# Order of the first transfers and a smaller activity credit in an attention and state-space kernel

## The chip, the core and the metric

The kernel runs on one NeuronCore of one Trainium2 chip. The metric is the device time of one execution in microseconds (us). Engine names are those of the profile: PE is the matrix engine, PEld its weight loads, DVE the vector engine, ACT the scalar engine, POOL and SP the other two. SP and ACT also issue transfers (DMAs); their issue rows are called SPq and ACTq.

## The reference

```python
g = sigmoid((x * gate_w).sum(-1, keepdims=True))          # x: 1 x 2048 x 512, bf16
# a: softmax attention with 32 heads of 16
q, k, v = split(x @ wqkv)
p = softmax(einsum("bhqd,bhkd->bhqk", q, k) * 16 ** -0.5)
a = einsum("bhqk,bhkd->bhqd", p, v) @ wo
# b: state-space convolution, 512 channels, 128 complex states each
dt = exp(log_dt);  A = A_re + 1j * A_im
K = einsum("dn,dnl,dn->dl", C, exp(dt * A * l), dt * B).real
b = causal_convolution(x, K) + x * Dskip                    # the reference uses an FFT
out = g * a + (1 - g) * b
```

## The kernel before

**Tiles and groups.** Attention is 32 heads by 16 key tiles (of 128 keys) by 4 query chunks (of 512 queries), which makes 2048 score tiles of 128 keys by 512 queries. They are worked off in 683 groups of three. For group `g`, `qk(g)` on PE writes the scores into one of two score buffers in PSUM (`SC0`, `SC1`); `ex(g)` on ACT takes the exponential of two or three of the tiles and writes them to `ET`; where ACT takes two, DVE makes the third by integer arithmetic on the bit pattern (`DZ`, `DU`). `pv(q)` on PE multiplies four finished tiles with the values (`VE`) into the PSUM bank `OA`. All other work stands between these: projections of later heads into the bank `MB`, the tables and the convolution kernel of the state-space part (DVE, PE), the convolution itself (PE), the normalization and the output product.

**What sets the order.** Each engine runs its instructions in the order in which `record` writes them, and waits on semaphores for what they need. A planner in `record` decides that order while it writes: it keeps an estimated clock for each engine, and after each `ex(g)` its method `fill` issues pieces of the other work that fit before the next group. Transfers have no planner: SP and ACT issue theirs in the order of the program.

**Activity and the fill.** The planner counts for PE how many columns the matmuls stream, weighted by the share of the 128x128 array that they use: a 512-column matmul on the whole array counts 512, one on a quarter of it (32 rows or 32 columns: `qk`, `pv`) counts 128. For each group it wants `FILL` = 1300 such columns per 1.335 us of ACT's estimated time. What is missing is made up by matmuls with a zero operand (`wm`), which add nothing: `zero` writes four of them side by side, of 512 or 256 columns each, into the accumulation bank in use (rows `OA<-wm` or `MB<-wm`), or into the next score buffer (`SC<-wm`). What a group has over or under its want is passed to the next in `lack`, within limits (lines of the kernel before):

```python
1607        t = p.tm["ACT"]
1608        want = FILL * (t - t0) / 1.335 + min(max(lack, -256), 768)
1609        t0 = t
1610        sch.fill(t, t + OVER, want)
1611        lack = want - p.act
1612        p.act = bare = 0
1613        while lack >= 256 and p.tm["PE"] < t + OVER:
1614            z = zbank()
1615            if z is None:
1616                bare = BARE
1617                break
1618            n = 512 if lack >= 512 else 256
1619            for j in range(4):
1620                zero(z, n, (0, 32 * j), 128, 32, n * ZCOL if j == 0 else 0, n // 4, "C")
1621            lack -= n
```

A negative `lack` is a surplus. Since less than 256 missing columns bring no fill, a surplus of 256 lets the next group run 256 plus almost 256 columns under 1300.

**The start.** `x0n` is the first quarter of x (512 rows, 512 KB), with rows on partitions; `ldt` is log_dt, repeated on all partitions; `Wq`, `Wk`, `Wv` are the parts of wqkv; `AimT`, `AreT`, `BreT` ... are the state-space parameters, transposed by the transfer; `xT` is x transposed, its chunks 1 to 3 by transposing transfers. Chunk 0 is made on PE: 16 matmuls `SC<-idb,x0n` and `MB<-idb,x0n` transpose `x0n`, and four copies (`CAST xT`, quarters `q4` = 0 to 3) bring it to `xT`, two on DVE and two on ACT. Before and after these PE runs 9 and 5 matmuls on zeros (`OA<-wm`, `SC<-wm` 128x512). Then come `bn` = `AimT` * `dt` and `ba` on DVE, the sine and cosine `sb_` and `cb` on ACT, the first projections (`OA<-xT,Wq`, `SC<-xT,Wk`), their copies (`Qm`, `KT`) on DVE, and `qk(0)`. ACT changes its function table for `dt` (exponential), `sb_` (sine) and the first `ET` (exponential).

The profile's lines 647 and 651 are those of the helpers `mm` and `load`, 662 and 666 those of `load_xT` and `load_par`, 928 that of `ex`, 964 that of `bits`. In the changed kernel all lines behind line 47 stand one lower, so 647 becomes 648.

Of the kernel before, what the change touches and what calls it, by code (L numbers as in the profile page):

```python
# [10 lines left out]
AF = mybir.ActivationFunctionType  # L11
ALU = mybir.AluOpType

P = 128
S = 2048
D = 512
# [28 lines left out]
RATE = 24.0  # L45
BURST = 48
FILL = 1300
OVER = 0.3
DLAG = .6
TURN = dict(F=.105, R=.105, C=.105, H=.06)  # L50
# [57 lines left out]
class Prog:  # L108
# [139 lines left out]
    def dma(self, eng, fn, R=(), W=(), c=.45, lat=3.0, m=DMARG):  # L248
        if self.cap is not None:
            self.cap.append((self.dma, (eng, fn, R, W), dict(c=c, lat=lat, m=m)))  # L250
            return
        self.log.append((self.dma, self.q, (eng, fn, R, W)))
        if eng == "POOL":
            k = NDSEM + self.pnext
            self.pnext = (self.pnext + 1) % NPSEM
        else:
            k = self.dnext
            self.dnext = (k + 1) % NDSEM
        s = ("D", k)
        deps = self._deps(s, R, W)  # L260
        if self.dn[k]:
            deps[s] = max(deps.get(s, -1), self.dn[k])
        at = self.tm[eng]
        for s2, k2 in deps.items():
            at = max(at, self.fin[(s2, k2)] + .08)
        self.tm[eng] = at + c
        self.dn[k] += 1
        self.fin[(s, self.dn[k])] = at + c + lat
        self.marg[(s, self.dn[k])] = m
        self._record(eng, fn, deps, s, self.dn[k], R, W)  # L270
# [352 lines left out]
def dap(t, off, dims):  # L623
    return bass.AP(tensor=t, offset=off, ap=[list(d) for d in dims])
# [6 lines left out]
def record(nc, p, B, ins):  # L631
# [6 lines left out]
    op, dma = p.op, p.dma  # L638
# [3 lines left out]
    x_t, w_t = ins["x"], ins["w"]  # L642
    MM, QUAD = .23, .22

    def mm(out, lhsT, rhs, R, W, start=True, stop=True, pos=None, c=MM, a=512, cfg="F"):
        kw = {} if pos is None else dict(tile_position=pos)
        op("PE", lambda t: t.matmul(out(), lhsT(), rhs(), start=start, stop=stop, skip_group_check=True, **kw), R, W,  # L647
           c=c, lat=.15, a=a, cfg=cfg)

    def load(eng, b, src, W, dims=None, off=0, c=.5, lat=4.5):  # L650
        dma(eng, lambda e: e.dma_start(b(off, dims), src()), [], W, c=c, lat=lat)
# [10 lines left out]
        dma("SP", lambda e: e.dma_start_transpose(xT(512 * c, [[S, 4], [1, 512]]),  # L662
                                                  dap(x_t, 512 * c * D, [[D, 512], [1, D]])), [], [(xT, c)], c=5.4, lat=1.5)

    def load_par(n, src, q="SP"):
        dma(q, lambda e: e.dma_start_transpose(B[n](0, [[1, D]]), src), [], [(B[n], 0)], c=1.25, lat=2.5)

    def load_w(n, c0, at, cols, sl, eng="ACT"):
        load(eng, B[n], lambda: dap(w_t, c0 + at, [[3 * D, P], [P * 3 * D, 4], [1, cols]]), [(B[n], sl)], [[D, 4], [1, cols]], at)

    load("SP", B["x0n"], lambda: dap(x_t, 0, [[D, P], [P * D, 4], [1, D]]), [(B["x0n"], 0)], [[D, 4], [1, D]])
    load("ACT", B["ldt"], lambda: dap(ins["ldt"], 0, [[0, P], [1, D]]), [(B["ldt"], 0)], [[1, D]])
    load_w("Wq", 0, 0, P, 0)
    load_w("Wk", D, 0, P, 0, "SP")
    load_par("AimT", ins["aim"])
    load_par("AreT", ins["are"])
    load_w("Wv", 2 * D, 0, D, 0, "SP")
    load_xT(1)
    load_w("Wk", D, P, D - P, 1, "SP")
# [11 lines left out]
    idf, idb, x0n = B["idf"], B["idb"], B["x0n"]  # L691
# [160 lines left out]
    def acts(g):  # L852
        return len(slots(g)) - (vec[g][2] if g in vec else 0)
# [31 lines left out]
    def at_slot(s):  # L885
        q, j = divmod(tiles[s], 4)
        b, kt = divmod(q, 16)
        return q, j, b, kt, (b % 8) // 2
# [136 lines left out]
    def key(*ns):  # L1025
        return [(B[n], 0) for n in ns]
# [499 lines left out]


    mb, oa = (MB, 0, 0), (OA, 0, 0)
    op("ACT", lambda a: a.activation(B["dt"](0, [[1, D]]), B["ldt"](0, [[1, D]]), AF.Exp), key("ldt"), key("dt"), c=.6)
    for q4 in range(4):  # L1530
        sc = SC[1] if q4 < 3 else MB
        off = 512 * (q4 % 3)
        sl = q4 % 3
        for i in range(4):
            mm(lambda sc=sc, off=off, i=i: sc(off + 128 * i, [[1, P]]), lambda q4=q4, i=i: x0n(D * i + P * q4, [[1, P]]),
               lambda: idb(0, [[1, P]]), [(x0n, 0), (idb, 0)], [(sc, sl, 'x0')], c=.07)
        R, W = [(sc, sl, 'x0')], [(xT, (0, q4))]
        if q4 % 2:
            op("ACT", lambda v, sc=sc, off=off, q4=q4: v.copy(xT(q4 * S, [[1, 512]]), sc(off, [[1, 512]])), R, W, c=.58)
        else:  # L1540
            op("DVE", lambda v, sc=sc, off=off, q4=q4: v.tensor_copy(xT(q4 * S, [[1, 512]]), sc(off, [[1, 512]])), R, W, c=.62)
    for k in range(5):
        mm(lambda: SC[0](512, [[1, 512]]), lambda: wm(0, [[1, 128]]), lambda: wm(0, [[1, 512]]), [(wm, 0)], [(SC[0], 1, "warm")])
    tt("DVE", full("bn"), full("AimT"), full("dt"), ALU.mult, key("AimT", "dt"), key("bn"), F5)
# [23 lines left out]
    def need(g):  # L1568
        for s in slots(g):
            q, j, b, kt, pi = at_slot(s)  # L1570
            sch.force(f"K{pi}.{kt // 4}")
            sch.force(f"qm{b}")

    ring = {}
    lack = t0 = bare = 0
    for g in range(NG):
        p.q = g
        if g == GKEEP:
            for n in ("gT", "zc"):
                B[n].last = g  # L1580
        for i in range(acts(g)):
            if held[g] + i in ring:
                sch.force(f"pv{ring[held[g] + i] // 4}")
            ring[held[g] + i] = tiles[3 * g + i]
        ex(g)
        sch.mark(f"g{g}")
        sch.mark(f"blk{at_slot(3 * g)[2]}")
        if g + 1 < NG:
            decide(g + 1)
            need(g + 1)  # L1590
            if g - 1 in vec:
                sch.force(f"bits{g - 1}")
            sc = SC[(g + 1) % 2]
            while lack >= 256 and bare:
                n = 512 if lack >= 512 else 256
                for j in range(4):
                    zero((sc, [(sc, 0, ("z", g + 1))]), n, (0, 32 * j), 128, 32, n * ZCOL if j == 0 else 0, n // 4, "C", True)
                lack -= n
                bare -= 1
            lack += p.act  # L1600
            qk(g + 1)
            if g + 1 in vec:
                i = sets[vec[g + 1][0]]["old"]
                if i is not None:
                    sch.force(f"dvp{i}")
                sch.add(bits(g + 1), 0)
        t = p.tm["ACT"]
        want = FILL * (t - t0) / 1.335 + min(max(lack, -256), 768)
        t0 = t
        sch.fill(t, t + OVER, want)  # L1610
        lack = want - p.act
        p.act = bare = 0
        while lack >= 256 and p.tm["PE"] < t + OVER:
            z = zbank()
            if z is None:
                bare = BARE
                break
            n = 512 if lack >= 512 else 256
            for j in range(4):
                zero(z, n, (0, 32 * j), 128, 32, n * ZCOL if j == 0 else 0, n // 4, "C")  # L1620
            lack -= n
        p.act = 0
# [24 lines left out]
    for i in range(4):  # L1647
        b, off, sl = banks[i]
        R, W = [(b, sl, ('o', 12 + i))], [(fo, i, 12 + i)]
# [39 lines left out]
```

## Time and profile before

| | |
|---|---|
| median of 3 runs | 809.06 us (807.52 to 810.83) |
| the profiled execution | 809.1 us, its span 807.3 us |
| mean granted clock of PE | 0.973 |
| busy in the span | ACT 780.6 us (97%), DVE 728.8 (90%), PE 696.1 (86%), PEld 277.2 (34%), POOL 11.7 |
| exponentials | 683 instructions, 772.1 us |

All times are counted from the start of the span. The profiled execution took as long as the median of the runs, within 0.1 us; 1.8 us of it lie outside the span. ACT is busy nearly all the time, so the places to look at are those where it is not: the start, the end and short waits between. A row of a timeline gives start, duration, engine, line, operation, output<-input and, in brackets, how long the engine sat idle before it and for what. A row of the stretches gives for each engine the busy time and the number of instructions, then the granted clock of PE (1.00 is full), the DMA share and GB/s.

### The profile page before, as it was taken

Reading aid. Unit: us, or ns where it says so; the run is one execution under the profiler, and the core shown is the slowest. Engines: PE = TensorE matmul, PEld = TensorE weight load, DVE = VectorE, ACT = ScalarE, POOL = GpSimd, SP = SyncE. Lnnn points to the kernel's source line nnn. Section 1 sums busy time; section 2 is a strip of 40 time slices with the busy share of each in tenths; the row PEclk is TensorE's granted clock in tenths of the full one; section 3 lists DMA queues with packets and bytes.
Section 4 is the critical chain, followed back from the end, with each engine's and each line's share of the span. In section 5 each row is a group of like instructions: output and inputs, shape, how many; then the busy total and the mean of one; then the engine's idle time right before and its main releaser. Section 6 shows DMA issues by size and latency. Waiting matters only on the chain.

```text
span 807.3 us, 27243 instructions
## 1 busy us (share of the span) xinstructions
PE 696.1 (86%) x12164; PEld 277.2 (34%) x12164; DVE 728.8 (90%) x1355; ACT 780.6 (97%) x695; POOL 11.7 (1%) x15
## 2 busy tenths in 40 slices
PE   7897878787788877778889999999999989999986
PEld 2322323323222434444434443443343432222221
DVE  5889999999699999989897889898989999999994
ACT  6999999999999999999999999999999999999995
POOL 5000000000000000000000000000000000000000
PEclk9969998999999999999999999999999999999999
DMA  8900000100531988877767899979897931000000
GB/s 193 166 2 17 9 15 15 30 12 14 152 105 44 208 193 214 205 172 185 205 145 177 211 225 202 207 179 178 190 188 160 181 74 29 19 17 24 18 7 28
DMA packets 115125, 93.17 MB, mean 115 GB/s; under 512 B 77760, under 2 KB 90432, under 8 KB 115008
## 3 DMA queue, kind: packets, MB, share of 16 engines
q1 hardware_dynamic: 114048, 90.91, 49.5%
q8 instruction: 95, 1.56, 0.9%
q10 hardware_dynamic: 960, 0.52, 0.3%
q14 instruction: 22, 0.18, 0.1%
HBM read 70.88 MB, written 13.97 MB: 105 GB/s over the span
## 4 chain that ended last, share of the span: by engine, by line
ACT 82%; PE 11%; DVE 4%; issue 1%; DMA 1%; ACTq 0%
ACT ET L928 82%; PE SC L647 5%; PE OA L647 3%; PE MB L647 3%; DVE DZ L964 1%; DMA x0n<-in_A_x_dram 1%; DVE PT L1020 0%; DVE ft L1020 0%; DVE ta L1020 0%; DVE KT L737 0%; DVE DZ L975 0%; DVE FP L1020 0%; DVE Yst L1337 0%; DVE At L1158 0%; DVE Kst L1245 0%
## 5 line engine op out<-in xcount | busy, mean ns | idle before, releaser
L928 ACT ACTIVATE ET<-SC 128x1024 bf16<-128x1024 f32 (+1 forms) x683 | 772.1, 1434 | 11.3 <-PE SC L647 6.9
L647 PE MATMUL SC<-Qm,KT 32*128 32x512 bf16 x2048 | 280.8, 391 | 85.8 <-ACT ET L928 72.5
L964 DVE TENSOR_SCALAR DZ<-SC 128x512 uint16<-128x512 f32 x348 | 230.2, 684 | 19.6 <-PE SC L647 18.8
L647 PE MATMUL OA<-ET,VE 128*32 128x512 bf16 x1700 | 170.6, 399 | 0.9 <-ACT ET L928 0.8
L647 PEld LDWEIGHTS SC<-Qm,KT 32*128 32x128 bf16 x2048 | 72.3, 91 | 269.2 <-ACT ET L928 232.2
L647 PE MATMUL OA<-wm 32*128 32x512 bf16 (+3 forms) x524 | 142.7, 389 | 1.2 <-DVE wm L695 1.2
L647 PE MATMUL MB<-Xop,Kf 128*64 128x64 bf16 (+1 forms) x4096 | 108.5, 196 | 3.9 <-issue 3.5
L647 PEld LDWEIGHTS MB<-Xop,Kf 128*64 128x64 bf16 (+1 forms) x4096 | 87.0, 104 | 51.1 <-issue 40.6
L647 PEld LDWEIGHTS OA<-ET,VE 128*32 128x32 bf16 x1700 | 43.0, 94 | 94.5 <-issue 90.5
L975 DVE TENSOR_SCALAR DZ<-DZ 128x2048 uint16<-128x2048 uint16 x87 | 59.4, 683 | 9.1 <-PE OA L647 9.0
L975 DVE TENSOR_SCALAR DU<-DZ 128x2048 uint16<-128x2048 uint16 x87 | 58.4, 684 | 0.2
L647 PEld LDWEIGHTS OA<-wm 32*128 32x128 bf16 (+2 forms) x524 | 34.6, 94 | 7.5 <-issue 6.2
L647 PE MATMUL OA<-DZ,VS 128*32 128x512 bf16 x348 | 34.8, 386 | 0.9 <-DVE DZ L975 0.9
L647 PE MATMUL OA<-DZ,VE 128*32 128x512 bf16 x348 | 34.3, 382 | 0.0
L647 PE MATMUL OA<-DU,VS 128*32 128x512 bf16 x348 | 34.3, 383 | 0.0
L647 PEld LDWEIGHTS MB<-PT,At 128*32 128x32 bf16 x2048 | 25.1, 95 | 10.3 <-issue 3.8
L647 PE MATMUL MB<-PT,At 128*32 128x64 bf16 (+1 forms) x2048 | 27.3, 189 | 0.3 <-issue 0.3
L1337 DVE TENSOR_TENSOR Yst<-MB,gt 128x512 bf16<-128x512 f32 x32 | 21.9, 684 | 4.8 <-PE MB L647 4.7
L1020 DVE TENSOR_TENSOR FP<-ft,ft 128x128 f32<-128x128 f32 (+1 forms) x64 | 22.8, 357 | 1.8
L999 DVE STREAM_TRANSPOSE OT<-OA 128x512 f32<-128x512 f32 x32 | 22.7, 710 | 1.7 <-PE OA L647 1.3
L647 PE MATMUL MB<-xT,Wk 128*128 128x512 bf16 x60 | 20.3, 428 | 0.3 <-DVE Kst L1245 0.3
L647 PE MATMUL MB<-Wv,xT 128*128 128x128 bf16 x256 | 20.3, 227 | 0.0
(227 smaller groups left out, 531.8 us busy)
## 6 DMA issues: line engine op xcount, KB each, us to landing
Xop<-gm_xpd SPq DMA_DIRECT2D x64, 320.0 KB, 4.7
Xop<-gm_xpd SPq DMA_DIRECT2D x64, 316.0 KB, 4.8
Kf<-gm_kpd SPq DMA_DIRECT2D x32, 376.0 KB, 5.4
Kf<-gm_kpd SPq DMA_DIRECT2D x32, 369.0 KB, 5.2
gm_ytd<-Yst SPq DMA_DIRECT2D x32, 128.0 KB, 4.2
gm_kpd<-Kst SPq DMA_DIRECT2D x32, 94.0 KB
gm_qd<-Qs SPq DMA_DIRECT2D x15, 128.0 KB, 1.7
Qm<-gm_qd SPq DMA_DIRECT2D x120, 16.0 KB, 3.3
```

Source lines behind the costliest of these rows:

```text
L647: op("PE", lambda t: t.matmul(out(), lhsT(), rhs(), start=start, stop=stop, skip_group_check=True, **kw), R, W, c=c, lat=.15, a=a, cfg=cfg)
L928: op("ACT", lambda a: a.activation(ET(512 * e, [[1, 512 * n]]), sc(0, [[1, 512 * n]]), AF.Exp, scale=DH ** -0.5), [(sc, i, g) for i in ran ...
L964: op("DVE", lambda v: v.tensor_scalar(z.u16(512 * k, [[1, 512 * n]]), sc(512 * na, [[1, 512 * n]]), XS, XBI, ALU.mult, ALU.add), [(sc, na ...
L975: op("DVE", lambda v: v.tensor_scalar(t.u16(0, [[1, 2048]]), z.u16(0, [[1, 2048]]), float(STEP[k][0]), None, ALU.add), R, W, c=.07 + 2048 ...
L999: op("DVE", lambda v: v.transpose(OT(512 * w, [[1, 512]]), OA(0, [[1, 512]])), [(OA, 0, b)], [(OT, w, b)], c=.64)
L1020: op(eng, lambda v: v.tensor_tensor(o(), a(), b_(), f), R, W, c=c)
L1337: op("DVE", lambda v, r2=r2: v.tensor_tensor(Yst(r2 * 512, [[64, 8], [1, 64]]), MB(0, [[64, 8], [1, 64]]), B["gt"](0, [[0, 8], [1, 64]]), ...
```

## The change

It has two parts. The first is the start: `x0n` and the first part of `Wk` move from SP's queue to ACT's, which now issues `x0n`, `ldt`, `Wq`, `Wk`; on SP `AimT` is first, and `AreT` waits until `x0n` has landed; all that follows on SP stands behind that wait. The exponential `dt` moves behind ACT's copy of `xT`, and the copy of quarter 3 moves from ACT to DVE. The second is the limit on the surplus that a group passes on: 128 columns in place of 256.

```diff
+CRED = 128
...
-    def load_par(n, src, q="SP"):
-        dma(q, lambda e: e.dma_start_transpose(B[n](0, [[1, D]]), src), [], [(B[n], 0)], c=1.25, lat=2.5)
+    def load_par(n, src, q="SP", R=()):
+        dma(q, lambda e: e.dma_start_transpose(B[n](0, [[1, D]]), src), R, [(B[n], 0)], c=1.25, lat=2.5)
...
-    load("SP", B["x0n"], lambda: dap(x_t, 0, [[D, P], [P * D, 4], [1, D]]), [(B["x0n"], 0)], [[D, 4], [1, D]])
+    load("ACT", B["x0n"], lambda: dap(x_t, 0, [[D, P], [P * D, 4], [1, D]]), [(B["x0n"], 0)], [[D, 4], [1, D]])
     load("ACT", B["ldt"], lambda: dap(ins["ldt"], 0, [[0, P], [1, D]]), [(B["ldt"], 0)], [[1, D]])
     load_w("Wq", 0, 0, P, 0)
-    load_w("Wk", D, 0, P, 0, "SP")
+    load_w("Wk", D, 0, P, 0)
     load_par("AimT", ins["aim"])
-    load_par("AreT", ins["are"])
+    load_par("AreT", ins["are"], R=[(B["x0n"], 0)])
...
-    op("ACT", lambda a: a.activation(B["dt"](0, [[1, D]]), B["ldt"](0, [[1, D]]), AF.Exp), key("ldt"), key("dt"), c=.6)
     for q4 in range(4):
...
-        if q4 % 2:
+        if q4 == 1:
             op("ACT", lambda v, sc=sc, off=off, q4=q4: v.copy(xT(q4 * S, [[1, 512]]), sc(off, [[1, 512]])), R, W, c=.58)
         else:
             op("DVE", lambda v, sc=sc, off=off, q4=q4: v.tensor_copy(xT(q4 * S, [[1, 512]]), sc(off, [[1, 512]])), R, W, c=.62)
+    op("ACT", lambda a: a.activation(B["dt"](0, [[1, D]]), B["ldt"](0, [[1, D]]), AF.Exp), key("ldt"), key("dt"), c=.6)
...
-        want = FILL * (t - t0) / 1.335 + min(max(lack, -256), 768)
+        want = FILL * (t - t0) / 1.335 + min(max(lack, -CRED), 768)
```

SP's queue at the start, before:

```order
L651 DMA x0n<-in_A_x_dram 128x4x512
L651 DMA Wk<-in_A_wqkv_dram 128x4x128
L666 DMA_TRANSPOSE AimT<-in_B_A_im_dram 128x512
L666 DMA_TRANSPOSE AreT<-in_B_A_re_dram 128x512
L651 DMA Wv<-in_A_wqkv_dram 128x4x512
L662 DMA_TRANSPOSE xT<-in_A_x_dram 128x4x512
```

The same queue now (`s_d0` is the semaphore that `x0n` raises when it has landed):

```order
L667 DMA_TRANSPOSE AimT<-in_B_A_im_dram 128x512
L667 DMA_TRANSPOSE AreT<-in_B_A_re_dram 128x512 [waits s_d0]
L652 DMA Wv<-in_A_wqkv_dram 128x4x512
L663 DMA_TRANSPOSE xT<-in_A_x_dram 128x4x512
L652 DMA Wk<-in_A_wqkv_dram 128x4x384
```

Two transfers left SP; behind the new wait the order is that of before.

ACT at the start, before:

```order
L651 DMA ldt<-in_B_log_dt_dram 128x512
L651 DMA Wq<-in_A_wqkv_dram 128x4x128
L1529 ACT_TABLE_LOAD
L1529 ACTIVATE dt<-ldt 128x512
L1539 CAST xT<-SC 128x512
L1539 CAST xT<-MB 128x512
L1545 ACT_TABLE_LOAD
L1545 ACTIVATE sb__121<-bn 128x512
```

ACT at the start, now:

```order
L652 DMA x0n<-in_A_x_dram 128x4x512
L652 DMA ldt<-in_B_log_dt_dram 128x512
L652 DMA Wq<-in_A_wqkv_dram 128x4x128
L652 DMA Wk<-in_A_wqkv_dram 128x4x128
L1539 ACT_TABLE_LOAD
L1539 CAST xT<-SC 128x512
L1542 ACTIVATE dt<-ldt 128x512
L1546 ACT_TABLE_LOAD
L1546 ACTIVATE sb__121<-bn 128x512
```

There are still as many table loads; `dt` stands behind a copy that needs `x0n`, and one copy (from `MB`) is gone.

PE in groups 9 and 10, before:

```order
L647 MATMUL SC<-Qm,KT 128x512 x3
L647 MATMUL OA<-ET,VE 32x512 x4
L647 MATMUL SC<-Qm,KT 128x512
L647 MATMUL OA<-wm 128x512
L647 MATMUL SC<-Qm,KT 128x512 x2
L647 MATMUL MB<-Wv,xT 128x128 x16
```

The same place now:

```order
L648 MATMUL SC<-Qm,KT 128x512 x3
L648 MATMUL OA<-ET,VE 32x512 x4
L648 MATMUL OA<-wm 32x256 x4
L648 MATMUL SC<-Qm,KT 128x512
L648 MATMUL OA<-wm 128x512
L648 MATMUL SC<-Qm,KT 128x512 x2
L648 MATMUL MB<-Wv,xT 128x128 x16
```

The first group here had three `qk` and four `pv`, 896 counted columns; it now has four zero matmuls of 256 columns more, 1152. Over the whole program the matmuls `OA<-wm 32x256` go from 84 to 232 and `OA<-wm 32x512` from 124 to 172, while `SC<-wm 32x512` go from 40 to 28 and `OA<-wm 128x512` from 316 to 314. Later pieces of work (projections above all) move by a few groups to and fro. The split of the score tiles between ACT and DVE is unchanged: ACT has 334 exponentials of three tiles and 349 of two in both.

## Prediction

> **What bounds the kernel.** I read the page first, then the stretches, then the chain of waits at the start.
>
> ```profile
> PE 696.1 (86%) x12164; PEld 277.2 (34%) x12164; DVE 728.8 (90%) x1355; ACT 780.6 (97%) x695; POOL 11.7 (1%) x15
> PEclk9969998999999999999999999999999999999999
> ACT 82%; PE 11%; DVE 4%; issue 1%; DMA 1%; ACTq 0%
> ```
>
> ACT bounds it: 780.6 of 807.3 us, and 82% of the chain of work that ended last. The change takes no exponential from ACT, so only the 26.7 us in which ACT is not busy can move. Where they lie (stretch, busy times, clock):
>
> ```profile
> 8.60:12.00 3.40, 3.40 (x9) 1.22 (x8) 1.79 (x4) 3.35 (x5) 3.40 (x3) 0.51 1.19 305
> 48.00:60.00 12.00, 12.00 (x111) 3.16 (x111) 9.38 (x23) 10.52 (x10) 0.00 (x0) 0.51 0.01 2
> 15.00:240.00 225.00, 181.76 (x2677) 66.50 (x2674) 201.12 (x403) 222.09 (x167) 0.00 (x0) 0.92 0.22 52
> 240.00:400.00 160.00, 129.07 (x3327) 63.48 (x3324) 150.19 (x310) 158.55 (x123) 0.00 (x0) 0.99 0.72 175
> 400.00:793.00 393.00, 366.35 (x6060) 139.78 (x6057) 364.53 (x607) 387.21 (x395) 0.00 (x0) 1.00 0.58 127
> ```
>
> ACT lost 2.91 us from 15 to 240, 1.45 to 400, 5.79 to 793; the rest is start and end. From 15 to 240 the clock averages 0.92, and half of the loss there (1.48 us) is one stretch, 48 to 60, at half clock with PE busy in all of it. So there are two places for the two parts: the start, and the half-clock stretches.
>
> **The start.** The chain up to the first exponential (its long pieces), PE's wait in it, and ACT beside it:
>
> ```profile
> 0.74 6.50 DMA x0n<-in_A_x_dram
> 8.35 1.81 PE SC L647 x5
> 10.16 1.71 PE OA L647 x4
> 11.87 0.99 PE SC L647 x4
> ```
> ```profile
> 7.28 0.84 PE L647 MATMUL SC<-idb,x0n 128*128 128x128 bf16 x12 [2.07 <-DMA x0n<-in_A_x_dram]
> ```
> ```profile
> 5.95 0.63 ACT L1529 ACTIVATE dt<-ldt 128x512 bf16<-128x512 bf16 x1 [2.98 <-DMA ldt<-in_B_log_dt_dram]
> 7.94 0.58 ACT L1539 CAST xT<-SC 128x512 bf16<-128x512 f32 x1 [1.36 <-PE SC L647]
> 9.03 1.28 ACT L1545 ACT_TABLE_LOAD   x1
> 10.32 0.63 ACT L1545 ACTIVATE sb__121<-bn 128x512 f32<-128x512 f32 x1
> 10.86 0.71 ACT L1547 ACTIVATE cb<-ba,hpi 128x512 f32<-128x512 f32 x1
> 11.59 1.28 ACT L928 ACT_TABLE_LOAD   x1
> 14.07 1.45 ACT L928 ACTIVATE ET<-SC 128x1536 bf16<-128x1536 f32 x1 [1.20 <-PE SC L647]
> ```
>
> `x0n` lands at 7.24 and the first exponential starts at 14.07, 6.83 us behind it. Below, x is the landing. Two strands run from x: PE's, which ended last, and ACT's, which was done at 12.87 (x+5.63) and waited 1.20 us.
>
> Landing. `x0n` shared its 6.5 us with `ldt`, `Wq`, `Wk` and two transposes. Now it is alone in front of ACT's queue, with `AimT` beside it, and the others behind it or behind its landing.
>
> ```profile
> x0n<-in_A_x_dram SPq DMA_DIRECT2D x1, 512.0 KB, 6.5
> ldt<-in_B_log_dt_dram ACTq DMA_DIRECT2D x1, 128.0 KB, 5.2
> Wk<-in_A_wqkv_dram SPq DMA_DIRECT2D x1, 384.0 KB, 4.1
> ```
>
> No row shows it in that place. The nearest is `ldt`, first on that queue at the same moment: 5.2 us, so x = 0.74 + 5.2, about 6.0, a gain of 1.2. Ends: `Wk`'s 384 KB in 4.1 us gives 4.8 (gain 2.4); 6.5 as before gives none. Nothing excludes a small loss, since `AimT` now starts 1.05 us earlier beside it; as the others' bytes are gone, I bound it by 0.3. The Trainium skill, DMA: Bandwidth & Descriptors, section "Issuing engines are not separate DMA queues", says that transfers from all issuing engines run on the same 16 DMA engines and interleave, and that using several saves only the time to issue. By that rule the move to ACT's queue is worth nothing in itself and all gain comes from what no longer runs beside `x0n`. The rows of before, with both queues mixed, do not tell the two apart, and the sum is 1.2 by either.
>
> From x on. ACT's strand: one copy to x+1.28 as before, `dt` 0.63 to x+1.95 (it ran before x until now), the table load 1.28 to x+3.23.
>
> ```profile
> 7.72 1.29 DVE L1541 CAST xT<-SC 128x512 bf16<-128x512 f32 x2 [3.78 <-PE SC L647]
> 8.92 0.68 DVE L1020 TENSOR_TENSOR bn<-AimT,dt 128x512 f32<-128x512 bf16 x1
> 9.64 0.69 DVE L1546 SCALAR_TENSOR_TENSOR ba<-bn 128x512 f32<-128x512 f32 x1
> ```
>
> DVE starts its copies at x+0.48; three of them at 0.645 end at x+2.42, `bn` at x+3.10, `ba` at x+3.8. So `sb_` starts with its table at x+3.23, `cb` ends near x+4.55, and the second table load ends at x+5.85, 0.22 later than now: the copy taken off ACT pays for most of `dt`. That is the floor of the first exponential. PE's strand was x+6.83 because its 13 matmuls of 512 columns (`SC<-wm` x5, `OA<-xT,Wq` x4, `SC<-xT,Wk` x4) ran at half clock (0.51 from 8.6 to 12.0), 0.43 us each. The clock fell after PE had stood for 2.07 us waiting for `x0n`; with x at 6.0 it stands for 0.8 us, so I expect the clock to hold and PE to save more than a microsecond. Then ACT's floor decides. I take x+6.1, near it, and 0.2 more since `ldt` now lands behind `x0n` while `dt` is wanted at x+1.3. First exponential: 6.0 + 6.3 = 12.3, **1.8 us earlier**. Ends: 4.8 + 5.85 = 10.65 (3.4 earlier), 7.5 + 6.83 = 14.3 (0.3 later).
>
> The new wait. Behind `AreT` on SP stand `Wv`, the chunks of `xT`, the rest of `Wk` and `Wq`, and the parameters.
>
> ```profile
> 3.78 2.38 SPq L666 DMA_TRANSPOSE AreT<-in_B_A_re_dram  x1
> 6.21 0.58 SPq L651 DMA_DIRECT2D Wv<-in_A_wqkv_dram  x1
> 14.16 1.07 PE L647 MATMUL MB<-Wv,xT 128*128 128x128 bf16 x16
> 15.57 0.39 PE L647 MATMUL SC<-Qm,KT 32*128 32x512 bf16 x3 [0.34 <-ACT ET L928]
> 16.74 0.63 ACT L1074 ACTIVATE ea<-an 128x512 f32<-128x512 f32 x1
> ```
>
> `AreT` goes out at 6.0 and takes at most 2.38 to issue, so `Wv` goes out by 8.4 (6.21 before), 2.2 us later. The first who waits is PE at `MB<-Wv,xT`, in order ahead of the `qk` of group 2. That `qk` ended at 15.96, while ACT, after `ea`, wanted it at 17.37: 1.4 us to spare. With the first exponential at 12.3 PE wants `Wv` at 12.4 and can wait until 13.8. By `Wk`'s 4.1 us it lands at 12.5, by `x0n`'s 6.5 at 14.9, when ACT waits 1.1 us. I take 4.1, the row of the same queue in mid-stream, so nothing. `AreT` itself is wanted only by `an` and `ea`, later still. The two transfers less on SP gain nothing.
>
> **The smaller credit.** Which groups get more work the order tells. Of the first 240 groups, those under 1150 counted columns fall from 73 to 40, where typical groups have 1300 or more. Does PE's clock follow that count? Two stretches at full clock, 3.4 us each, the first just ahead of the half clock:
>
> ```profile
> L647 PE MATMUL SC<-Qm,KT 32*128 32x512 bf16 x9 | 1.3, 426 | 0.4 <-ACT ET L928 0.3
> L647 PE MATMUL OA<-ET,VE 128*32 128x512 bf16 x4 | 0.4, 390 | 0.0
> ...
> L647 PE MATMUL MB<-gwT,xT 128*128 128x1 bf16 x8 | 0.4, 165 | 0.0
> L647 PE MATMUL OA<-wm 128*32 128x256 bf16 x4 | 0.3, 283 | 0.0
> ```
> ```profile
> 42.70:46.10 3.40, 2.33 (x34) 0.87 (x30) 3.33 (x7) 3.40 (x4) 0.00 (x0) 1.00 0.00 0
> ```
> ```profile
> L647 PE MATMUL MB<-xT,Wk 128*128 128x512 bf16 x6 | 1.6, 383 | 0.0
> L647 PE MATMUL OA<-ET,VE 128*32 128x512 bf16 x8 | 0.8, 391 | 0.0
> L647 PE MATMUL SC<-Qm,KT 32*128 32x512 bf16 x6 | 0.8, 384 | 0.7 <-ACT ET L928 0.6
> ```
>
> From 42.7 to 46.1 PE is busy 2.33 of 3.40 us, but with quarter-array work: 22 such matmuls of 512 columns (9 of them, all fill, in the rows left out) and 4 of 256 count 3080 with the gate's 8. The rows of 70.0 to 73.4 count 4864, and in this slice of the page (60 to 81 us) the clock stays at 9 tenths or more, against 6 in the slice before. So it follows the weighted count, not the busy time. The Trainium skill, TensorE: Matmul & The Clock Gate, section "HAM oscillation — how this bites in real kernels", gives the rule as no idle gaps of PE over about 3.4 us. By that rule this kernel would never lose its clock in mid-course; the 0.51 from 48 to 60, with no such gap ahead of it, disagrees.
>
> Gain: half-clock stretches cost at most ACT's 2.91 us. The 1.48 us of 48 to 60 follow groups with gate matmuls whose content the change leaves as it is, so whether it comes back is chance: I take a quarter, 0.4. Of the other 1.43, the share of low groups that vanishes, 33 of 73: 0.6. Together **1.0 us**, ends 2.9 and 0. Cost: 184 more zero matmuls, 46 sets of four. A set takes 0.28 us with 256 columns by the row above and 0.39 with 512 (the `pv` row), 13 to 18 us in all, beside PE's 43 us of free time from 15 to 240. At full clock that is cover enough: nothing. At half clock there is none (12.00 of 12.00).
>
> **Sum.** 809.1 - 1.8 - 1.0 = **806.3 us**, against the profiled execution, which stands at the median (809.06). From 240 on, where the order is only shuffled, I count nothing.
>
> **Rivals.**
> 1. Both parts at their good ends: `x0n` at 4.8 to 5.4 with the clock held, and hardly a half-clock stretch left: 2.9 + 2.7 less, 803.5 us. For it: what shared the transfer is gone, and the low groups are nearly halved.
> 2. The fill does not do what it says: the half-clock stretches move but stay as many, because the clock answers to something else than the counted columns, or because the low groups that remain suffice. Then only the start counts: 809.1 - 1.8 = 807.3 us. For it: the groups ahead of the longest stretch are unchanged; against it: the two counts above. The Trainium skill's rule on idle gaps, from the page and section named above, would make it this one.
> 3. `x0n` lands no earlier, because the first transfer is slow by itself (`ldt` took 5.2 us for a quarter of the bytes), or `ldt` comes so late behind it that `dt` eats the gain: 809.1 - 1.0 = 808.1 us.
> 4. `Wv` late behind the new wait: 6.5 us, 1.1 us lost, 807.4 us.
> 5. Slower: the fill is load where the clock is halved. A mean clock of 0.92 means 16% of the 225 us at half clock, so 7 of the 46 sets, each 0.28 us or, at half speed, double that: 2 to 4 us on the end if the stretches stay. It decides above 6 sets at 0.28, which eat the 1.8 us of the start: 809.3 to 811.3, say 810.3. Against it: more columns should also bring the clock back sooner.
>
> **Chances.** Forecast 0.40 (own range 805.0 to 807.3), rival 1 0.20, rival 2 0.16, rival 3 0.11, rival 4 0.05, rival 5 0.08. The range 803.2 to 809.0 leaves out rival 5 and about half of rival 1. A difference of 0.5%, 4.0 us, is about what a measurement can tell from no change. Faster by that, under 805.0, is rival 1 and the forecast's lower fringe: 0.25. Slower, over 813.1: 0.03. The rest, 0.72, is the same.
>
> **What would show it.** In the trace after: `x0n` landing near 6.0 after issue on ACTq at 0.74; clock 1.00 over the `OA<-xT,Wq` matmuls; ACT's second table load ending just ahead of the first `ET`, near 12.3; no idle time of PE ahead of `MB<-Wv,xT`; a clock over 0.92 and less than 2.91 us lost on ACT from 15 to 240. I am wrong if `ET` waits for a transfer, if the clock from 15 to 240 is no higher, or if ACT's losses behind 240 grow from the 7.24 us of now by more than one.

## The result and the profile after

The changed kernel took 803.24 us (median of 19 runs, 798.32 to 811.54), the kernel before 809.76 (19 runs beside them). The ratio is 0.9927, with a 95% interval of 0.9906 to 0.9948: 6 us less. Twelve more runs of the changed kernel later gave 805.09 us and 0.9957 (0.9927 to 0.9986). Ratios and means leave out the runs that took over 1.5% more than the fastest of their kernel (one of the 19 and one of the 12), which count as a slower state. The forecast was 806.3, its range 803.2 to 809.0.

The profiled execution took 804.18 us, its span 802.4 (before: 807.3), at a mean granted clock of 0.982 (0.973). From its page, busy times, clock slices, and the chain that ended last:

```profile
PE 696.8 (87%) x12346; PEld 277.7 (35%) x12346; DVE 731.3 (91%) x1356; ACT 778.8 (97%) x694; POOL 11.8 (1%) x15
PEclk9999999999999999999999999999999898999999
```

ACT still bounds it. The clock's slices that were at 6 and 8 tenths are at 9 or more, and two behind 620 us are now at 8. The chain up to the first exponential, its long pieces in order of time (start, duration, what):

```profile
1.19 4.02 PE OA L648 x9
5.21 0.87 PE SC L648 x8
6.10 0.59 ACT xT L1539
6.68 0.53 ACT dt L1542
7.23 1.28 ACT L1546
8.52 0.63 ACT sb__121 L1546
9.15 0.61 ACT cb L1548
9.77 1.28 ACT L929
11.07 1.24 ACT ET L929
```

It begins with PE's nine matmuls on zeros, not with a transfer. The first transfers, from issue to landing:

```profile
x0n<-in_A_x_dram ACTq DMA_DIRECT2D x1, 512.0 KB, 4.0
...
ldt<-in_B_log_dt_dram ACTq DMA_DIRECT2D x1, 128.0 KB, 4.6
```

`x0n` was issued at 0.74 and landed near 4.75 (7.24 before), half a microsecond before the last zero matmul ended at 5.21. Two rows of SP and two of PE on the new wait:

```profile
4.78 1.14 SPq L667 DMA_TRANSPOSE AreT<-in_B_A_re_dram  x1
5.97 0.58 SPq L652 DMA_DIRECT2D Wv<-in_A_wqkv_dram  x1
```
```profile
7.50 1.03 PE L648 MATMUL OA<-xT,Wq 128*128 128x512 bf16 x4
...
10.86 1.07 PE L648 MATMUL MB<-Wv,xT 128*128 128x128 bf16 x16
```

`AreT` went out as soon as `x0n` was there, took 1.14 us to issue in place of 2.38, and `Wv` was issued at 5.97, even 0.24 earlier than before. `MB<-Wv,xT` has no idle time in front of it. The stretches (columns as before):

```profile
8.60:12.00 3.40, 2.39 (x26) 1.18 (x24) 3.36 (x9) 3.38 (x4) 2.45 (x2) 1.00 1.11 268
...
48.00:60.00 12.00, 10.03 (x116) 3.30 (x116) 11.43 (x27) 12.00 (x11) 0.00 (x0) 1.00 0.05 14
```
```profile
15.00:240.00 225.00, 177.83 (x2810) 66.17 (x2809) 203.70 (x406) 224.81 (x170) 1.35 (x1) 0.99 0.22 52
240.00:400.00 160.00, 130.81 (x3406) 63.88 (x3410) 150.33 (x309) 158.57 (x125) 0.00 (x0) 0.98 0.73 180
400.00:792.11 392.11, 371.94 (x6041) 140.36 (x6037) 363.18 (x605) 384.09 (x391) 0.00 (x0) 0.98 0.58 125
```

The last stretch ends with the last exponential, at 792.11 (796.83 before). The balance of this pair of profiles: the first exponential starts 3.0 us earlier (11.07 for 14.07); ACT loses 0.19 us from 15 to 240, where it lost 2.91, so 2.7 less; behind 240 it loses 1.43 + 8.02 = 9.45 for 7.24, 2.2 more; the exponentials themselves took 771.0 us for 772.1. Together 4.6 of the 4.7 us by which the last exponential ends earlier. What was given back has a place, the 15 us from 630 on, first before and then after:

```profile
630.00:645.00 15.00, 14.10 (x314) 6.54 (x310) 14.05 (x26) 14.41 (x15) 0.00 (x0) 1.00 0.91 158
```
```profile
630.00:645.00 15.00, 12.79 (x213) 4.86 (x206) 10.29 (x18) 11.14 (x12) 0.00 (x0) 0.77 0.91 189
```

ACT lost 3.86 us there in place of 0.59. Part of it only moved: in the 15 us behind, ACT had lost 1.80 us before and now lost none. Over both, first before and then after, the loss grew from 2.39 to 3.86:

```profile
630.00:660.00 30.00, 27.71 (x586) 12.25 (x578) 28.36 (x49) 27.61 (x30) 0.00 (x0) 1.00 0.71 130
```
```profile
630.00:660.00 30.00, 27.35 (x481) 10.74 (x473) 24.17 (x40) 26.14 (x28) 0.00 (x0) 0.89 0.74 152
```

In the chain that ended at that place, SP issues a transposing transfer (`Yt`, line 1352) ahead of a load of `Xop` (line 1280), and PE waits for the load:

```profile
626.98 1.28 SPq L1352
...
628.30 0.59 SPq L1280
...
628.99 5.57 DMA Xop<-gm_xpd
...
634.60 1.18 PE MB L648 x17
635.78 0.54 PE SC L648 x3
```

The `qk` behind those `MB` matmuls come late, and ACT waits up to 2.6 us at a time. This place lies in the body, not in the start; which of the two brings the loss is tested below.

The profile read by itself would say: 3.0 us from the start, 2.7 from the smaller credit, 2.2 given back further on. The experiments had to test this, since one execution had gone into it.

### The profile page after: what moved, and what is told of

Its sections match the earlier page's. It is cut to its first block, busy times and chain, and to the rows that moved or that the text cites. A ratio compares the mean times of both kernels' runs of the same rounds, so it can differ in the third digit from the quotient of the medians.

```text
span 802.4 us, 27602 instructions
## 1 busy us (share of the span) xinstructions
PE 696.8 (87%) x12346; PEld 277.7 (35%) x12346; DVE 731.3 (91%) x1356; ACT 778.8 (97%) x694; POOL 11.8 (1%) x15
## 4 chain that ended last, share of the span: by engine, by line
ACT 88%; PE 7%; DVE 2%; issue 1%; DMA 1%; SPq 0%; ACTq 0%
ACT ET L929 87%; PE SC L648 3%; PE OA L648 3%; PE MB L648 2%; DMA Xop<-gm_xpd 1%; DVE DZ L965 1%; SPq L1352 0%; DVE ft L1021 0%; DVE FP L1021 0%; DVE OT L1000 0%; ACT L929 0%; ACT L1546 0%; ACT fo L1652 0%; DVE At L1159 0%; DVE Kst L1246 0%
## 5 line engine op out<-in xcount | busy, mean ns | idle before, releaser
L929 ACT ACTIVATE ET<-SC 128x1024 bf16<-128x1024 f32 (+1 forms) x683 | 771.0, 1483 | 9.6 <-PE SC L648 7.7
L648 PE MATMUL OA<-wm 128*32 128x256 bf16 (+3 forms) x718 | 155.6, 360 | 2.5 <-issue 1.3
L648 PE MATMUL MB<-Xop,Kf 128*64 128x64 bf16 (+1 forms) x4096 | 110.2, 197 | 4.3 <-issue 2.7
L648 PEld LDWEIGHTS MB<-Xop,Kf 128*64 128x64 bf16 (+1 forms) x4096 | 88.7, 105 | 51.7 <-issue 40.1
L648 PEld LDWEIGHTS OA<-wm 128*32 128x32 bf16 (+2 forms) x718 | 39.8, 94 | 11.4 <-issue 10.1
L648 PE MATMUL MB<-PT,At 128*32 128x48 bf16 (+1 forms) x2048 | 27.9, 190 | 1.4 <-issue 1.4
L1021 DVE TENSOR_TENSOR At<-ta,ta 128x512 bf16<-128x512 bf16 x48 | 18.5, 419 | 0.6
```

The source lines that it names most:

```text
L929: op("ACT", lambda a: a.activation(ET(512 * e, [[1, 512 * n]]), sc(0, [[1, 512 * n]]), AF.Exp, scale=DH ** -0.5), [(sc, i, g) for i in ran ...
L1021: op(eng, lambda v: v.tensor_tensor(o(), a(), b_(), f), R, W, c=c)
```

## The experiments

Each kernel ran beside the kernel before on the same chip. "First exponential" is the start of the first `ET` in the profiled execution (14.07 before, 11.07 after).

### The two parts apart

The start alone, twice, 6 and 12 runs; the second time beside the changed kernel itself:

```diff
-CRED = 128
+CRED = 256
```

> The changed kernel with the old credit of 256 columns. Theory: the two parts are worth about 3 us each and add up; the start stays at its new length (first exponential near 11.1 us), while the half-clock stretches come back: 70 of the first 240 groups are under 1150 counted columns (40 in the changed kernel), the clock from 15 to 240 us falls towards 0.92 to 0.95 and ACT loses 2 to 3 us there. Time 3 us under the kernel before, 806 to 807. Rival: the credit does nothing to the clock and the body of the changed kernel won by its shuffled order alone: the clock from 15 to 240 stays near 0.99 and the time is that of the changed kernel, 803 to 804.

> The changed kernel with the old credit of 256 (the start alone), run side by side with the changed kernel itself. So far the start alone took 800.8 us (6 runs) and both parts 803.2 (19 runs). Theory (the smaller credit is worth nothing, or costs a little because it shuffles the order of the body): 801 to 803 us, not slower than the changed kernel beside it. Rival (the credit brings its 1 us after all, and the 800.8 were six lucky executions): 1 us or more slower than the changed kernel beside it, about 804.

> The changed kernel itself once more, on the same chip and in the same rounds as the start alone. Theory (credit worth nothing): 803 to 804 us, level with the start alone or up to 2 us slower. Rival (credit worth 1 us): 1 us or more faster than the start alone.

Measured: the start alone took 800.76 us, ratio 0.9903 (0.9870 to 0.9937), and the second time 803.96, 0.9938 (0.9910 to 0.9966). The changed kernel beside the second took 805.09, 0.9957 (0.9927 to 0.9986). The first expectation, 806 to 807 us at a clock of 0.92 to 0.95 from 15 to 240, missed. So the start alone is not slower than both parts: the means are 802.9 us (18 runs) against 803.7 (29 runs), and their standard errors 0.7 and 0.5. The credit of 128 brings no gain that shows.

Then the credit alone in the kernel before, and no credit at all with the new start:

```diff
-        want = FILL * (t - t0) / 1.335 + min(max(lack, -256), 768)
+        want = FILL * (t - t0) / 1.335 + min(max(lack, -128), 768)
```

> The kernel before with the credit of 128 columns and the old start. Theory: first exponential near 14 us as before, 43 of the first 240 groups under 1150 counted columns (73 before), clock from 15 to 240 us at 0.97 or more and under 1 us lost by ACT there; time 2 to 3 us under the kernel before, 806.5 to 807.5. Rival (the credit does nothing): clock 0.92 to 0.95 there, time as before, 809 to 810. Rival (the fill is load): slower than before.

```diff
-CRED = 128
+CRED = 0
```

> The changed kernel with no credit at all: 19 of the first 240 groups stay under 1150 counted columns (40 with 128, 70 with 256). Theory: the clock from 15 to 240 us is 0.99 to 1.00 in nearly every execution, but little is left to win there (0.2 us in the profile of the changed kernel), so the time is that of the changed kernel or up to 1.5 us less, 801.5 to 803.5. Rival (more fill is load on PE): ACT waits for PE and the time is 1 us or more above the changed kernel.

Measured: the credit alone 808.25 us, ratio 0.9994 (0.9967 to 1.0021), the first exponential at 13.82. Its profile had a clock of 0.98 from 15 to 240 and lost 1.09 us there, much as expected, but lost 3.62 us from 240 to 400 (before: 1.45). Without credit 809.78, 1.0011 (0.9985 to 1.0036), with the first exponential at 11.40: the start's gain was there, and all of it was lost in the body. By the planner's count few groups were left under 1150 columns there (19 of the first 240; 40 in the changed kernel, 73 before), and yet one stretch from 44 to 61 us ran at half clock. That was the expectation's clearest miss: fewer low groups did not mean a higher clock.

```profile
15.00:240.00 225.00, 179.91 (x2948) 68.70 (x2959) 197.12 (x394) 221.94 (x166) 0.00 (x0) 0.95 0.26 62
```

ACT lost 3.06 us here, at a clock of 0.95.

### The same program, two executions

The stretch 15 to 240 of the start alone, from its first and its second profile, and of the changed kernel from its second:

```profile
15.00:240.00 225.00, 173.51 (x2708) 65.64 (x2724) 202.38 (x404) 223.86 (x169) 1.35 (x1) 0.98 0.22 53
```
```profile
15.00:240.00 225.00, 179.27 (x2690) 65.76 (x2704) 198.58 (x397) 221.71 (x166) 1.35 (x1) 0.92 0.22 52
```
```profile
15.00:240.00 225.00, 182.82 (x2755) 66.06 (x2768) 196.90 (x394) 220.48 (x165) 1.35 (x1) 0.91 0.20 51
```

The same program with the same 70 low groups had a clock of 0.98 once and 0.92 once. The changed kernel had 0.99 in the profile above and 0.91 here, and ACT lost 0.19 us there and 4.52 here, 2.40 of it in a half-clock stretch from 44 to 64. So the 2.7 us that the first pair of profiles shows between 15 and 240 lies within what one program does from one execution to the next, and cannot be put down to the credit. The traces show how close it was. With the matmuls' columns counted over steps of 3.41 us from the clock's first record, weighted as the planner weights them, the changed kernel's first profile held 3120 to 3571 in the four steps from 40 to 54 and kept its clock; its second held 3088 in the step ahead of 43.6, the clock fell, and the next six steps held 2330 to 2966. What repeats is the loss further back: in this second profile ACT lost 3.49 us from 630 to 645, against 3.86 in the first, with the same `Xop` load in the chain.

```profile
630.00:645.00 15.00, 11.97 (x250) 5.67 (x242) 10.88 (x19) 11.51 (x12) 0.00 (x0) 0.86 0.84 179
```

### Start and body exchanged, instruction by instruction

An edit of the source makes the planner reorder the whole body, so none of the runs above holds the body still. Three more do. In the first two the finished program of one kernel is kept, and only the instructions of the start are changed in it:

```diff
-        log = prog.log
+        log = start(prog.log, bufs)
```

`start` gives the program of before the new start (`x0n` and `Wk` on ACT, the wait of `AreT`, the copy of quarter 3 on DVE, `dt` behind the copies), or the changed program the old one. In the third, the program of before stays word for word and gets 43 sets of four zero matmuls of 256 columns, where a credit of 128 would have asked for one (`also` counts what that credit would pass on):

```diff
+        also = FILL * (t - t0) / 1.335 + min(max(also, -128), 768)
...
+        z = zbank() if also >= 256 and p.tm["PE"] < t + OVER else None
+        if z is not None:
+            also -= 256
...             (four zero matmuls of 256 columns, not counted by the planner)
```

> The new start (transfers, wait, dt and the copy moved) with everything else issued in the order of the kernel before, row by row; the credit is that of before. Theory A (the start is worth what the profiles show, the rest of the start-only kernel's gain is its shuffled order): first exponential near 10.8 to 11.1, time 3 us under the kernel before at a like mean clock, 805.5 to 806.5. Theory B (the start also keeps the clock up later): mean clock 0.98 as in the start-only kernel (0.973 before) and the time 5 us or more under before, 802 to 804.

> The old start with everything else in the changed kernel's order and with its fill. Theory A (start and order are separate): 3 us over the changed kernel at a like mean clock, 806 to 807, so 2 to 3 us under the kernel before. Theory C (the start is all of the change's gain): as the kernel before, 809 to 810, first exponential near 14.

> The kernel before, row by row, with 43 more sets of four zero matmuls of 256 columns behind groups that a credit of 128 would have filled; no other instruction moves. Low groups among the first 240 fall from 73 to 43. Theory of the prediction (the clock answers to the counted columns): mean clock up from 0.973 to 0.98 or more, at a like clock no slower than before, time 1.5 to 2.5 us less, 806.5 to 808. Rival (fill is load): mean clock no higher, time as before or up to 2 us more, 809 to 811. Rival (both, and they cancel): mean clock 0.98, but slower at a like clock by 1 us or more, time as before.

Measured, 12 runs each:

| start | body | us | ratio (95%) | first exponential |
|---|---|---|---|---|
| new | before's | 805.50 | 0.9951 (0.9926 to 0.9977) | 10.66 |
| old | changed | 808.61 | 1.0004 (0.9979 to 1.0030) | 14.12 |
| old | before's + 43 sets | 807.07 | 0.9986 (0.9965 to 1.0007) | 13.99 |

The new start in the old body gives 4.0 us (1.9 to 6.0), and the new body with the old start gives nothing that shows (1.7 us faster to 2.4 slower). That is the verdict on the two parts: the start carries the gain that can be shown. The fill alone brings 1.1 us, but its interval includes none. It does no harm: rival 5, the slower one, is out, at least for 43 sets in this body. The changed body with the old start, from 15 to 240:

```profile
15.00:240.00 225.00, 179.36 (x2768) 66.30 (x2780) 199.01 (x398) 222.64 (x168) 1.35 (x1) 0.94 0.23 52
```

ACT lost 2.36 us, with a half-clock stretch from 46 to 63 and all the fill of the smaller credit in place. From 630 to 645 it lost 3.38 us, with an `Xop` load in the chain as in both profiles of the changed kernel: that loss belongs to the body. From 630 to 660 all four profiles of the changed body (the fourth is the next section's first) lost 3.86 to 4.55 us; the old body with the new start lost 2.39, as before.

### Why x0n lands early

Three more kernels (one execution each) show the transfers. In the first, all four stand on SP, `x0n` first:

```diff
-    load("ACT", B["x0n"], ...
-    load("ACT", B["ldt"], ...
-    load_w("Wq", 0, 0, P, 0)
-    load_w("Wk", D, 0, P, 0)
+    load("SP", B["x0n"], ...
+    load("SP", B["ldt"], ...
+    load_w("Wq", 0, 0, P, 0, "SP")
+    load_w("Wk", D, 0, P, 0, "SP")
```

> The changed kernel with its four first transfers in the same order on SP instead of ACT, ahead of the transposes. Theory (what counts is what runs beside x0n, not the queue): x0n lands 4.0 to 4.5 us after its issue, as in the changed kernel, where it was 6.5 before; the first exponential near 11.1 us. Rival (ACT's queue starts moving earlier than SP's): x0n lands 5.3 us or more after its issue, first exponential at 11.7 or later.

In the second, the order on ACT is `ldt`, `x0n`, `Wq`, `Wk`:

```diff
-    load("ACT", B["x0n"], ...
     load("ACT", B["ldt"], ...
+    load("ACT", B["x0n"], ...
```

> The changed kernel with ldt ahead of x0n on ACT's queue. Theory (ldt, one row read 128 times, was the slow company): x0n lands 5.8 us or later after the first issue, near the old 6.5, though nothing else runs beside it. Rival (it was the bytes of the others, Wq, Wk and AreT, beside x0n): ldt's 128 KB cost about a quarter of x0n's own time, and x0n lands 4.8 to 5.3 us after the first issue.

In the third, `AreT` does not wait:

```diff
-    load_par("AreT", ins["are"], R=[(B["x0n"], 0)])
+    load_par("AreT", ins["are"])
```

> The changed kernel without the wait of AreT for x0n, so AreT and Wv go out at once on SP behind AimT. Theory (what is kept away from x0n is what counts): AreT and Wv run beside x0n, which takes 5 us or more in place of 4.0 and lands after the ninth zero matmul, at 5.8 or later; first exponential 11.6 or later. Rival (only ldt ahead or beside is harmful): x0n lands by 5.2 as before, the first exponential at 11.1, and the wait is not needed.

The transfers of the first, from issue to landing:

```profile
x0n<-in_A_x_dram SPq DMA_DIRECT2D x1, 512.0 KB, 3.8
```

of the second:

```profile
x0n<-in_A_x_dram ACTq DMA_DIRECT2D x1, 512.0 KB, 6.4
...
ldt<-in_B_log_dt_dram ACTq DMA_DIRECT2D x1, 128.0 KB, 4.6
```

and of the third:

```profile
x0n<-in_A_x_dram ACTq DMA_DIRECT2D x1, 512.0 KB, 4.0
...
ldt<-in_B_log_dt_dram ACTq DMA_DIRECT2D x1, 128.0 KB, 5.6
```

The queue does not matter: 3.8 us on SP, 4.0 on ACT. The Trainium skill, DMA: Bandwidth & Descriptors, section "Issuing engines are not separate DMA queues", says that all issuing engines' transfers run on the same 16 DMA engines; here the trace agrees. What matters is `ldt`, as far as one execution of each can tell. Issued 0.4 us ahead of `x0n` on one queue it makes `x0n` take 6.4 us, nearly the 6.5 of before, where `ldt` was issued at the same moment on another queue. Issued 0.5 us behind, it leaves `x0n` at 4.0, even where `AimT`, `AreT` and `Wv` go out at once on SP. So the new wait protects nothing of `x0n`, against the expectation of the third. It helps `ldt` a little. Without it `ldt` landed at 6.84, `dt` waited 0.68 us for it, and the first exponential started at 11.34, 0.27 later than in the changed kernel's first profile:

```profile
5.59 0.58 ACT L1539 CAST xT<-SC 128x512 bf16<-128x512 f32 x1 [1.47 <-PE SC L648]
6.86 0.63 ACT L1542 ACTIVATE dt<-ldt 128x512 bf16<-128x512 bf16 x1 [0.68 <-DMA ldt<-in_B_log_dt_dram]
```

The second also parts the head's gain: with `ldt` first, `x0n` landed at 7.52, 0.28 later than before, and still the first exponential came 0.78 earlier (13.29). So the rest of the new start (`dt` and the copy moved) together with the full clock is worth about 1 us of it; these two were not parted.

The times were 806.13, 821.21 and 802.71 us. The first has the changed kernel's body word for word on PE, DVE and POOL (and its loss from 630 to 645, 4.43 us); one execution does not tell it from the changed kernel. The other two have bodies that the planner ordered anew, so their times say little of the transfers. In the 821 us, ACT lost 12.65 of 225 us from 15 to 240, with half-clock stretches at 37, 50 and 81 us among others; why this body does so badly, or whether only that execution did, is open.

### Fewer zeros at the start

Since nine zero matmuls ended behind the landing, seven were tried, with the credit of 256:

```diff
-    for k in range(9):
+    for k in range(7):
```

> The start alone (credit 256), with 7 in place of 9 matmuls on zeros ahead of the transposes of x0n. In the profile of the changed kernel x0n landed at 4.76 while the ninth zero matmul ended at 5.21, so the zeros and not the transfer set the start. Theory: two zeros of 0.43 us less let the transposes begin at the landing, 4.6 to 4.9, and the first exponential comes 0.3 to 0.5 us earlier than with nine, near 10.4; 0.4 us less in all, which the time can hardly show. Rival: fewer zeros leave the clock at half over the transposes and the first projections, 0.4 to 0.9 us more, and the first exponential is no earlier than 10.7.

Measured: 810.60 us in 12 runs, ratio 1.0034 (1.0005 to 1.0062), 6.6 us more than the start alone in the same rounds. Neither theory had that. The first exponential was at 10.64, against 10.71 with nine zeros in the profile beside it: the transposes began with the landing of `x0n` in both (4.90 and 5.01), so there was nothing to win, and the 12 transposes took 0.89 and 0.84 us, so no clock was lost. The loss is behind the start. Two zeros less change the planner's estimate of PE, and soon after the start the projections and the fill stand in other groups. From 240 to 400:

```profile
240.00:400.00 160.00, 130.70 (x3220) 64.10 (x3221) 144.79 (x300) 155.13 (x120) 0.00 (x0) 0.94 0.73 180
```

ACT lost 4.87 us there; in the start alone it lost none in one profile and 1.55 in the other. Over the 12 runs the mean clock was 0.969, against 0.977 for the start alone. A body ordered by chance is worth as much as the change itself.

## Why the prediction was right, and where it was not

**What bounds it, and the head's floor: right.** ACT still bounds the kernel. The prediction set the first exponential's floor at x + 5.85 by ACT's strand. In both profiles of the start alone, where the chain begins with `x0n` (landed at 5.01 and 4.97), it started at x + 5.75 and x + 5.74. In the changed kernel's profile it started at x + 6.32, behind the second table load that ended at 11.05; 0.46 of that lies between the landing and 5.21, when PE had ended its zeros. The copy, `dt`, the two table loads, `sb_` and `cb` stood in the order and with the durations that the sum had. The extra 0.2 for a late `ldt` was not needed: `dt` followed the copy without idle time.

**Landing: a mis-sized term.** The step "The nearest is `ldt`, first on that queue at the same moment: 5.2 us, so x = 0.74 + 5.2, about 6.0" took the wrong row. `ldt` is the slow transfer itself (4.0 to 5.6 us for 128 KB in all positions tried), and the one that slowed `x0n`. The lower end, taken from `Wk`'s 384 KB in 4.1 us, was the answer: 3.8 to 4.6 us in all profiles with `x0n` ahead of `ldt`. Rival 3 is out. With x at 4.75, PE's zeros at 5.21 became the bound in this profile, which the prediction had not named. The head brought 3.0 us in this pair of profiles, and 2.7 to 3.4 over those with `x0n` ahead of `ldt` (first exponential at 10.64 to 11.40), where it counted 1.8.

**The clock in the head: right in what it expected, not shown in its reason.** The clock was 1.00 over `OA<-xT,Wq`. It was not yet full over the transposes, though the column reads 1.00: the trace's records of the clock begin at 6.09, and until then matmuls of 512 columns started 0.43 us apart, as they did before at 0.51. The changed kernel's transposes and those of the start alone (second profile):

```profile
5.00 1.36 PE L648 MATMUL SC<-idb,x0n 128*128 128x128 bf16 x12
```
```profile
5.01 0.84 PE L648 MATMUL SC<-idb,x0n 128*128 128x128 bf16 x12 [0.16 <-DMA x0n<-in_A_x_dram]
```

The first record lies between 4.17 and 5.03 in five profiles with `x0n` ahead of `ldt` whose first exponential is at 10.64 to 10.76, and at 6.03 to 6.41 in the three with 11.07 to 11.40 (in the last, without credit, `x0n` landed later too, at 5.30; the kernel without the wait, late for `ldt`, aside). So the moment at which the clock first becomes full, which differs between executions, is worth some 0.4 us of the head.

The reason given, that PE had stood 2.07 us, does not hold by itself: with `ldt` first PE stood 2.37 us and the clock stayed full.

```profile
7.57 0.84 PE L648 MATMUL SC<-idb,x0n 128*128 128x128 bf16 x12 [2.37 <-DMA x0n<-in_A_x_dram]
```
```profile
8.60:12.00 3.40, 2.84 (x14) 1.08 (x11) 3.37 (x7) 3.35 (x6) 2.44 (x2) 1.00 0.58 142
```

The Trainium skill, TensorE: Matmul & The Clock Gate, section "HAM oscillation — how this bites in real kernels", allows gaps up to about 3.4 us; this trace agrees, and the one of before, half clock behind 2.07 us, does not. The weighted columns do tell the two apart: in the step of 3.41 us from the first record on they came to 2914 before, where the clock then fell, and to 4060 with `ldt` first.

**The new wait: right.** `Wv` was issued at 5.97, not at up to 8.4, since `AreT` took 1.14 us; nobody waited for it in this profile. In the second of the start alone and without credit PE waited 0.29 and 0.20 us for it, and ACT not at all. Rival 4 did not happen.

**The credit: the step that failed.** The terms "the share of low groups that vanishes, 33 of 73: 0.6" and "I take a quarter, 0.4" took the half-clock stretches of one profile for a property of the order of the groups. They vary between executions of one program (0.19 and 4.52 us lost), and with the old start the smaller credit's body gave 1.0004 (0.9979 to 1.0030). The fill by itself may be worth the forecast's microsecond (0.9986, 0.9965 to 1.0007), not more than about three: with the program of before word for word, the 43 sets went with a mean clock of 0.979 (12 runs) against 0.973 (29 runs beside them), a difference of 0.006 with a standard error of 0.002. In the order that the planner makes of the credit, nothing of it shows in the time. Rival 2's number, the start alone, fits this part; its first reason, that the clock answers to something else than the counted columns, does not; its second, that the low groups that remain suffice, does.

That the clock follows the weighted count, the traces bear out. Each of the 14 was cut into steps of 3.41 us from its first record of the clock, and the matmuls' columns in each step counted, weighted by their share of the array. Between 15 and 790 us, 3039 steps ran at full clock. Behind the 2838 with more than 3101 counted columns the clock never fell; behind the 201 with fewer it fell 86 times. (Some matmul records are missing, as the counts of one program, x12346 and x12310, show, so some of the low steps held more.) Unweighted columns part them worse: 693 of the steps that held had no more than the highest that fell, against 115. So does standing time: 1227 of the steps that held had as much of it as the least that fell, 0.52 us.

So the rule was right, and the fill thins the low steps, but one profile cannot show by how much. From 15 to 240 there were 6 to 12 low steps at full clock in the four profiles with a credit of 256 (mean 8.0, ACT lost 2.64 us there on average), 1 to 8 in the six with the fill of 128 (mean 5.3, 1.93 us), and 4 without credit.

**Nothing from 240 on: wrong by its own test.** The losses behind 240 grew from 7.24 to 9.45 us, more than the one that the prediction set as its mark. An `Xop` load behind a transposing transfer on SP stands in the chain of all four profiles of this body, which lost 3.38 to 4.43 us from 630 to 645. It stands also in both of the start alone, which lost 2.55 and 1.31 us from 630 to 660 (before: 2.39): the planner's new order brings it with either credit, and not always at a cost.

**The sum.** 809.1 - 1.8 - 1.0 came within 3.1 us of the first median and within 1.2 of the repeat, by two errors that nearly cancel: the head 1.2 too small, and the credit's 1.0, of which nothing shows in the time. That the sum came so near is luck in that respect. The first 803.24 lies 3 us below what the start explains (809.1 - 3.0 = 806.1), the repeat's 805.09 one below. The interval of the start in the old body, 1.9 to 6.0 us, covers that; no cause beyond the start is shown for it. The first median lies where rival 1 stood (803.5), and the first profile met its two conditions, `x0n` at 4.75 and hardly a half-clock stretch; the second profile did not meet the latter.

## What to carry to other kernels

Ask of a late first transfer what was issued at the same moment or just ahead of it, not on which queue it stands; here a 128 KB load repeated on all partitions cost the 512 KB load beside it 2.5 us, and half a microsecond's lead avoided it. Where a planner orders the rest, an edit at the start reorders everything behind it, by up to 6 us here: keep the finished program and exchange only the edited instructions before crediting the edit. One profile against one profile cannot price a change of a few microseconds in a kernel whose clock steps vary from execution to execution; the losses that repeat in several profiles can be priced.

## What the runs showed of the hardware

The granted clock of one program differs between executions: its mean had a standard deviation of 0.006 to 0.011 over the runs of a kernel, and over all runs a mean clock lower by 0.01 went with a span longer by about 2.6 us. A spread of some 10 us between runs of one kernel goes mostly with that: with the clock taken into account, 1.4 us of standard deviation remain, of 2.0 to 3.6.

In these traces the clock falls only behind a step of 3.41 us with about 3100 or fewer columns, weighted by their share of the array (86 falls of 201 such steps, none of 2838 others). The half-clock stretches last 3.41 us or a multiple of it (6.83, 13.65, 17.07, 20.48, 23.89) in all profiles, but for the one that the program's end cuts off. The long ones, 13.65 us and more, lie between 38 and 71 us, in eight of the fourteen profiles, with the old start and the new. What keeps the count low there was not tried.

`ldt`, 128 KB whose one row is repeated on 128 partitions, took 4.0 to 5.6 us, in each profile longer than the 512 KB of `x0n` issued ahead of it (3.8 to 4.6). Why the repeated row is slow was not tried.
